# Attention of two batches in front of gate and val of batch 0, with gate and val weights fetched from memory for each batch

## The chip, the cores and the metric

The kernel runs on one core of one Trainium2 chip. The metric is device time in microseconds (us). PE is TensorE, DVE VectorE, ACT ScalarE, POOL GpSimd. A "record" is one entry of the trace; the 48 matmuls of gate and val of batch 0 stand there as 96 records. A line number such as L407 is a line of the kernel whose profile is shown; the same code has other numbers in other kernels: gate and val matmuls are L382 before and L407 after, the output projection of batch 0 is L468 and L493, the making of v L356 and L381, the first matmuls of batch 1 L420 and L445.

## The reference

Eight batches (8 heads, 512 positions, 64 wide) attend to 32 states each, and the states attend to the positions. The 544 rows of a batch go through RMS norm and a SwiGLU layer. The weights arrive in float64.

```
scores = scale * x @ state.T ; a = softmax(scores) ; xread = a @ state
a2 = softmax(scale * state @ x.T)                  ; sread = a2 @ x
x = concat(xread, sread)  -> rows of 512
xn = x / sqrt(mean(x*x) + 1e-6) * rms_g
out = (silu(xn @ w_gate) * (xn @ w_val)) @ w_out   # d_ff = 1536
```

## The kernel before

DVE and ACT turn the weights into float32, 18 pieces of 128x1024: twelve of gate and val (a gate and a val piece make a pair `mp`), six of w_out. For batch 0 the kernel multiplies the states into a pair of gate and val (`make_v`), then the attention weights into that (`hidden`, twelve tiles numbered from 0, also called hidden tiles, 3.5 us of PE each), then projects (`project_as_ready`, 42 us of PE). Batches 1 to 7 use seven products in place of eight. Attention is a generator; each `next` or `some(n)` emits its next steps, which end up between the other work.

```python
def to_float32(k):                      # 5 DVE and 3 ACT operations a piece (cut)
    ...
    VE.tensor_scalar(ex, hi, 20, 0x7ff, ...)              # L158
    VE.tensor_scalar(top, hi, 0xfffff, 0x100000, ...)     # L164
    VE.scalar_tensor_tensor(out=man, in0=top, ...)        # L165
    VE.scalar_tensor_tensor(out=ex, in0=hi, ...)          # L167
    VE.tensor_tensor(out=dst, in0=man, in1=ex, op=ALU.mult)   # L171

steps = attention(0)
while next(steps) != "tokens":
    pass
make_v(0, 0)
ready(4)                                # four pieces converted
for _ in steps:
    pass

for b in range(B):
    steps = attention(b + 1) if b + 1 < B else state_norm()
    if b == 0:
        for m in range(NM):
            if m % 2 == 0 and m + 2 < NM:
                make_v(b, m // 2 + 1)
            hidden(m, S, ...)
        def between(m):                 # called at even m of the projection
            some(5)
            if m == NM - 4:
                ready(len(pieces)); early.close(); open_late()
                some(20)
                prepare(b + 1)
        project_as_ready(store_tokens(b), between)
    else:
        ...                             # seven products (cut)
```

Of the kernel before, what the change touches and what calls it, by code (L numbers as in the profile page):

```python
# [8 lines left out]
F32 = mybir.dt.float32  # L9
# [7 lines left out]
P = 128  # L17
RAW_AHEAD = 4


@with_exitstack
def kernel(
# [35 lines left out]
    one = ctx.enter_context(tc.tile_pool(name="one", bufs=1))  # L58
    two = ctx.enter_context(tc.tile_pool(name="two", bufs=2))
    aps = ctx.enter_context(tc.tile_pool(name="aps", bufs=2, space=PSUM))  # L60
    vps = ctx.enter_context(tc.tile_pool(name="vps", bufs=2, space=PSUM))
# [19 lines left out]
    def load_x(b, queue):  # L81
        x_sb[b] = one.tile([P, NC, H * D], F32, name="x_b")
        for c in range(NC):
            queue.dma_start(
                out=x_sb[b][:, c].rearrange("p (h d) -> p h d", h=H),
                in_=x[b, :, P * c:P * c + P, :].rearrange("h p d -> p h d"))
# [4 lines left out]
    GE.memset(mhalf, -0.5)  # L91
    ones = consts.tile([P, P], F32, name="ones")
    GE.memset(ones, 1.0)
# [5 lines left out]

    w = consts.tile([P, NI, NM, 2, P], F32, name="w")  # L100
    wo = consts.tile([P, NM, DM], F32, name="wo")
# [4 lines left out]
    for mp in range(NM // 2):  # L106
        for k, dram in enumerate((moe_w_gate, moe_w_val)):
            pieces.append((w[:, :, 2 * mp:2 * mp + 2, k, :],
                           dram[:, 2 * P * mp:2 * P * mp + 2 * P].rearrange("(i p) f -> p i f", p=P)))
    for mp in range(NM // 2):  # L110
        pieces.append((wo[:, 2 * mp:2 * mp + 2].rearrange("p m (i f) -> p m i f", f=P),
                       moe_w_out[2 * P * mp:2 * P * mp + 2 * P].rearrange("(m p) f -> p m f", p=P)))
    raw = {}

    def load_piece(k):
        if k >= len(pieces):
            return
        dst, src = pieces[k]
        if src.dtype == F32:
            src = src.rearrange("p a (c f) -> p a c f", f=P)  # L120
            for a in range(src.shape[1]):
                nc.sync.dma_start(out=dst[:, a], in_=src[:, a])
            return
        raw[k] = raws.tile([P, 8 * P, 2], I32, name="raw")
        out_ = raw[k].rearrange("p (a f) two -> p a (f two)", a=src.shape[1])
        for a in parts(k):
            nc.sync.dma_start(out=out_[:, a], in_=src[:, a].bitcast(I32))

    def parts(k):

        n = pieces[k][1].shape[1]
        return (slice(0, n // 2), slice(n // 2, n)) if k == 0 else (slice(0, n),)
# [3 lines left out]
    def ready(n):  # L136

        nonlocal n_ready
        while n_ready < min(n, len(pieces)):
            to_float32(n_ready)  # L140
            n_ready += 1

    def to_float32(k):


        load_piece(k + RAW_AHEAD)
        if k not in raw:
            return
        whole = raw.pop(k)
        tops = conv.tile([P, 8 * P], I32, name="top")  # L150
        exs = conv.tile([P, 8 * P], I32, name="ex")
        n = pieces[k][1].shape[1]
        for a in parts(k):
            cols = slice(8 * P * a.start // n, 8 * P * a.stop // n)
            r, top, ex, dst = whole[:, cols, :], tops[:, cols], exs[:, cols], pieces[k][0][:, a]
            hi = r[:, :, 1]
            man = r.bitcast(F32)[:, :, 0]
            VE.tensor_scalar(ex, hi, 20, 0x7ff, op0=ALU.logical_shift_right, op1=ALU.bitwise_and)  # L158

            SE.activation(out=ex, in_=ex, func=ACTF.Relu, scale=-1.0, bias=bounds[:, 0:1])  # L160
            SE.activation(out=ex, in_=ex, func=ACTF.Relu, scale=-float(1 << 23),
                          bias=bounds[:, 1:2])
            SE.activation(out=man, in_=r.bitcast(U32)[:, :, 0], func=ACTF.Copy, scale=2.0 ** -52)
            VE.tensor_scalar(top, hi, 0xfffff, 0x100000, op0=ALU.bitwise_and, op1=ALU.bitwise_or)  # L164
            VE.scalar_tensor_tensor(out=man, in0=top, scalar=2.0 ** -20, in1=man,  # L165
                                    op0=ALU.mult, op1=ALU.add)
            VE.scalar_tensor_tensor(out=ex, in0=hi, scalar=-(1 << 31), in1=ex,  # L167
                                    op0=ALU.bitwise_and, op1=ALU.bitwise_or)
            man, ex = (t.rearrange("p (a c f) -> p a c f", f=P, c=dst.shape[2])
                       for t in (man, ex.bitcast(F32)))  # L170
            VE.tensor_tensor(out=dst, in0=man, in1=ex, op=ALU.mult)  # L171
# [15 lines left out]
    def attention(b):  # L187
        xb, packed = x_sb.pop(b), rows.pop(b)
        if b + 1 < B:
            load_state(b + 1)  # L190

        stT = two.tile([P, 4, Ns], F32, name="stT")
# [19 lines left out]
        for j in range(4):  # L212
            for e in range(2):
                TE.matmul(out=sp[e][Ns * j:Ns * j + Ns, :], lhsT=stT[D * e:D * e + D, j, :],  # L214
                          rhs=xT[j // 2][D * e:D * e + D, j % 2].rearrange("p c t -> p (c t)"),
                          start=True, stop=True)
        sS = one.tile([P, 2, NC, P], F32, name="sS", tag="sS")
        e2 = one.tile([P, 2, NC, P], F32, name="e2", tag="xT0")
        s2 = two.tile([P, 2], F32, name="s2")
# [9 lines left out]
        for cp in range(2):  # L229
# [11 lines left out]
            yield  # L241
        aT = one.tile([P, 2, NC, P], F32, name="aT")
        for cp in range(2):
# [32 lines left out]
        for c in range(NC):  # L276
            TE.matmul(out=sp[:, c:c + 1], lhsT=sq[0][:, 0, P * c:P * c + P], rhs=ones[:, 0:1],  # L277
                      start=True, stop=True)
# [3 lines left out]
        rp = inverse_rms(ss, NC)  # L282
        aT_s[b] = two.tile([P, 2, S], F32, name="aT_s")
        VE.tensor_tensor(out=aT_s[b], in0=aT.rearrange("p e c t -> p e (c t)"),
                         in1=rp.unsqueeze(1).to_broadcast([P, 2, S]), op=ALU.mult)
# [10 lines left out]
        yield  # L296
        e2T = one.tile([P, 2, NC, P], F32, name="e2T", tag="eS")
        for e in range(2):
# [17 lines left out]
        for e in range(2):  # L316
            VE.tensor_scalar(sr[:, D * e:D * e + D], rp[:, e, :], z2[:, e:e + 1], None,
                             op0=ALU.mult)
        if b + 1 < B:
            load_x(b + 1, nc.sync)  # L320
        tp = aps.tile([P, 4, Ns], F32, name="at")
# [4 lines left out]
    def state_norm():  # L326

        sq = one.tile([P, NI, NT], F32, name="sqT", tag="eS")
        SE.activation(out=sq, in_=xsT, func=ACTF.Square, scale=DM ** -0.5)
        sp = aps.tile([P, NT // P], F32, name="at")  # L330
        for r in range(NT // P):
            for i in range(NI):
                TE.matmul(out=sp[:, r:r + 1], lhsT=sq[:, i, P * r:P * r + P], rhs=ones[:, 0:1],
                          start=(i == 0), stop=(i == NI - 1))
        ss = two.tile([P, NT // P], F32, name="sst")
        VE.tensor_scalar(ss, sp, 1e-6, None, op0=ALU.add)
        rp = inverse_rms(ss, NT // P)
        for i in range(NI):
            VE.scalar_tensor_tensor(out=xsT[:, i, :], in0=xsT[:, i, :], scalar=rms_g[:, i:i + 1],
                                    in1=rp[:, 0:NT], op0=ALU.mult, op1=ALU.mult)  # L340
        yield
# [8 lines left out]
    def make_v(b, mp):  # L350

        ready(2 * mp + 2)
        pv = [vps.tile([P, 4 * P], F32, name="pv") for e in range(2)]
        for j in range(4):
            for e in range(2):
                TE.matmul(out=pv[e][Ns * j:Ns * j + Ns, :],  # L356
                          lhsT=stT_g[b][D * e:D * e + D, j, :],
                          rhs=w[D * e:D * e + D, j, 2 * mp:2 * mp + 2].rearrange(
                              "p m k f -> p (m k f)"),
                          start=True, stop=True)  # L360
        v = two.tile([P, 2, 2, 2, P], F32, name="v")
        for e in range(2):
# [229 lines left out]
    ready(4)  # L592
    for _ in steps:
        pass
# [4 lines left out]

    for b in range(B):  # L600
        steps = attention(b + 1) if b + 1 < B else state_norm()
        if b == 0:
            for m in range(NM):
                if m % 2 == 0 and m + 2 < NM:
                    make_v(b, m // 2 + 1)
                v, _ = v_sb[b, m // 2]
                hidden(m, S, lambda e, k: v[:, e, m % 2, k, :],
                       [aT_s[b][:, e, :] for e in range(2)])

            def between(m):  # L610
                some(5)
                if m == NM - 4:
                    ready(len(pieces))
                    early.close()
                    open_late()
                    some(20)
                    prepare(b + 1)

            project_as_ready(store_tokens(b), between)
            sums = weight_sums()  # L620
        else:
            pairs = [hidden_seven(b, mp) for mp in range(NM // 2)]
# [15 lines left out]
    for m in range(NM):  # L638
        hidden(m, NT, lambda i, k: w[:, i, m, k, :], [xsT[:, i, :] for i in range(NI)])
    project_seven(NT, store_states, lambda: None, lambda: None)  # L640
# [30 lines left out]
```

## Time and profile before

| | before |
|---|---|
| median time in the rounds with the changed kernel | 879.43 us (878.08 to 880.06, 4 runs) |
| PE busy | 827.5 of 877.2 us |
| PE idle before batch 1 (161.2 us) | 34.5 us |
| PE idle from batch 1 to the end (716.0 us) | 15.2 us |
| last piece of weights converted | 136.2 us |

"Busy" says that an engine had work, not that the work was fast: at a granted clock of 0.50 sixteen matmuls for v take 2.44 us, at 1.00 they take 1.09. The sum "idle plus extra busy" is therefore what a stage has lost, and it is used below. The main lines stand in the prediction. One view more is the list of PE's waits from 60 to 165 us (columns: total us, times, longest us). It names who ended each wait. Its first three lines are shown; the four left out are of 0.7 us and less:

```profile
PE f L382 <- ACT v L363: 5.5, 3, 2.4
PE at L277 <- DVE sq L274: 1.8, 1, 1.8
PE at L184 <- POOL ri L181: 0.8, 1, 0.8
```

The first line is the conversion arriving just in time: gate and val wait for v, which waits for weights. The other two are attention of batch 1, which runs between matmuls of the projection.

### The profile page before, as it was taken

How to read it: one execution, taken by the hardware profiler on the slowest of the kernel's cores; microseconds unless marked ns; L12 is line 12 of the kernel's file. 1: busy time of each engine (PE TensorE's matmuls, PEld its weight loads, DVE VectorE, ACT ScalarE, POOL GpSimd, SP SyncE). 2: the span in 40 equal slices, each digit the busy share in tenths (PEclk: the TensorE clock that was granted, in tenths of full speed). 3: DMA queues.
4: the chain of work that ended last, by engine and by line, in shares of the span. 5: the costliest groups of instructions: out<-in, count | busy, mean ns of one | idle time of the engine just before them, and what ended most of it. 6: DMA issues, size and time to landing. Idle time of an engine off the chain costs nothing.

```text
span 877.2 us, 11950 instructions
## 1 busy us (share of the span) xinstructions
PE 827.5 (94%) x4806; PEld 607.1 (69%) x4806; DVE 473.5 (54%) x749; ACT 341.2 (39%) x571; POOL 150.9 (17%) x215
## 2 busy tenths in 40 slices
PE   3598898999999999999999999999999999999998
PEld 2143343577877778777877787777877787788886
DVE  5889997269216941476226921694148623651231
ACT  5667771464125520562136412552056313520110
POOL 0000003131113211230123112221132022310000
PEclk9589999999999999999999999999999999999999
DMA  9455412100210002000200021001100000001000
GB/s 284 156 145 182 157 48 49 48 1 4 50 48 2 1 21 67 13 1 4 72 25 1 4 50 47 1 1 36 50 13 1 1 25 25 1 1 37 13 0 25
DMA packets 53815, 37.47 MB, mean 43 GB/s; under 512 B 37888, under 2 KB 45568, under 8 KB 53760
## 3 DMA queue, kind: packets, MB, share of 16 engines
q1 hardware_dynamic: 49600, 35.66, 13.9%
q10 hardware_dynamic: 4160, 1.05, 0.6%
q8 instruction: 38, 0.62, 0.3%
q14 instruction: 17, 0.14, 0.1%
HBM read 27.79 MB, written 8.91 MB: 42 GB/s over the span
## 4 chain that ended last, share of the span: by engine, by line
PE 72%; issue 11%; DVE 9%; ACT 5%; DMA 1%; POOL 0%; ACTq 0%; POOLq 0%
PE f L511 30%; PE f L420 24%; PE f L382 5%; PE pv L356 4%; PE f L468 2%; PE at L206 2%; ACT sq L270 1%; PE at L214 1%; ACT e L294 1%; PE at L277 1%; PE at L264 1%; DVE m L290 1%; DVE hb L450 1%; DVE hb L446 1%; DVE sq L273 1%
## 5 line engine op out<-in xcount | busy, mean ns | idle before, releaser
L420 PE MATMUL f<-aT_s,v 128*128 128x256 f32 x504 | 131.9, 393 | 2.8 <-ACT g L437 2.8
L511 PE MATMUL f<-wo,hb 128*128 128x256 f32 x540 | 128.5, 396 | 0.0
L420 PEld LDWEIGHTS f<-aT_s,v 128*128 128x128 f32 x504 | 89.4, 189 | 52.9 <-issue 29.8
L511 PEld LDWEIGHTS f<-wo,hb 128*128 128x128 f32 x540 | 107.0, 200 | 17.6 <-ACT ot L531 1.9
L531 ACT COPY ot<-f 128x256 f32<-128x256 f32 x60 | 19.6, 375 | 195.6 <-PE f L511 190.3
L363 ACT COPY v<-pv 128x512 f32<-128x512 f32 x96 | 51.7, 591 | 106.6 <-PE pv L356 106.6
L511 PE MATMUL f<-wt,hs 128*128 128x256 f32 x360 | 88.8, 392 | 0.0
L371 POOL TENSOR_TENSOR vs<-v 128x256 f32<-128x256 f32 x42 | 30.6, 730 | 330.5 <-ACT v L363 330.5
L420 PE MATMUL f<-aT_t,vs 128*128 128x256 f32 x336 | 86.3, 379 | 0.0
L435 DVE TENSOR_TENSOR g<-g,f 128x512 f32<-128x512 f32 x42 | 28.7, 683 | 90.2 <-PE f L420 72.1
L511 PEld LDWEIGHTS f<-wt,hs 128*128 128x128 f32 x360 | 65.2, 191 | 16.4 <-issue 4.9
L536 DVE TENSOR_TENSOR ot<-ot,f 128x256 f32<-128x256 f32 x45 | 17.0, 417 | 104.9 <-issue 53.5
L420 PEld LDWEIGHTS f<-aT_t,vs 128*128 128x128 f32 x336 | 63.8, 190 | 9.5 <-issue 0.8
L356 PE MATMUL pv<-w,stT_g 64*32 64x512 f32 x768 | 64.7, 619 | 4.0 <-ACT sq L270 2.7
L445 ACT ACTIVATE hb<-g 128x1024 f32<-128x1024 f32 x42 | 44.4, 1057 | 34.8 <-DVE g L439 34.8
L446 DVE SCALAR_TENSOR_TENSOR hb<-hb,g 128x1024 f32<-128x1024 f32 x42 | 51.5, 1225 | 7.6 <-ACT hb L445 7.6
L181 POOL TENSOR_TENSOR ri<-ss,mhalf 128x4 f32<-128x4 f32 x8 | 8.9, 1113 | 237.9 <-DVE ss L280 196.7
L382 PE MATMUL f<-aT_s,v 128*128 128x512 f32 x96 | 43.3, 604 | 5.5 <-ACT v L363 5.5
L468 PE MATMUL f<-wo,hb 128*128 128x512 f32 x96 | 43.5, 597 | 0.0
L420 PE MATMUL f<-aT_t,v 128*128 128x256 f32 x168 | 43.1, 379 | 0.0
L420 PE MATMUL f<-aT_s,vs 128*128 128x256 f32 x168 | 43.1, 379 | 0.0
L382 PE MATMUL f<-xsT,w 128*128 128x256 f32 x192 | 41.6, 379 | 0.0
(114 smaller groups left out, 1244.7 us busy)
## 6 DMA issues: line engine op xcount, KB each, us to landing
x_b<-in_x_dram SPq DMA_DIRECT2D x28, 256.0 KB, 4.4
out_dram<-ot SPq DMA_DIRECT2D x56, 128.0 KB, 1.8
raw<-in_moe_w_val_dram SPq DMA_DIRECT2D x6, 1024.0 KB, 5.3
raw<-in_moe_w_out_dram SPq DMA_DIRECT2D x6, 1024.0 KB, 4.7
raw<-in_moe_w_gate_dram SPq DMA_DIRECT2D x5, 1024.0 KB, 5.2
x_b<-in_x_dram ACTq DMA_DIRECT2D x4, 256.0 KB, 5.2
raw<-in_moe_w_gate_dram SPq DMA_DIRECT2D x2, 512.0 KB, 6.0
out_dram<-ot SPq DMA_DIRECT2D x4, 256.0 KB, 2.0
```

Source lines behind the costliest of these rows:

```text
L206: TE.transpose(out=tp[:, c, :], in_=xb[:, c, P * j:P * j + P], identity=ident)
L356: TE.matmul(out=pv[e][Ns * j:Ns * j + Ns, :], lhsT=stT_g[b][D * e:D * e + D, j, :], rhs=w[D * e:D * e + D, j, 2 * mp:2 * mp + 2].rearrange ...
L363: SE.copy(v[:, e].rearrange("p m k f -> p (m k f)"), pv[e])
L371: GE.tensor_tensor(out=vs[:, 0], in0=a21, in1=a22, op=ALU.add)
L382: TE.matmul(out=ps[:, 0:n], lhsT=lhs(i, k), rhs=r, start=(i == 0), stop=(i == len(rhs) - 1))
L420: TE.matmul(out=ps[:, i, :], lhsT=lhs[:, i, :], rhs=rhs, start=(start and i == 0), stop=True, skip_group_check=True)
L435: VE.tensor_tensor(out=g[:, :, 0, :], in0=g[:, :, 0, :], in1=ys, op=ALU.add)
L445: SE.activation(out=h, in_=gate, func=ACTF.Tanh, scale=0.5)
L446: VE.scalar_tensor_tensor(out=h, in0=h, scalar=1.0, in1=gate, op0=ALU.add, op1=ALU.mult)
L468: TE.matmul(out=op, lhsT=hb[:, m, P * r:P * r + P], rhs=wo[:, m, :], start=(m == 0), stop=(m == NM - 1))
L511: TE.matmul(out=ps[:, r, :], lhsT=lhs(k)[:, P * r:P * r + P], rhs=rhs(k), start=(start and r == 0 and k == 0), stop=(k == HM - 1), skip_gr ...
L531: SE.copy(kept[r], ps[:, r, :])
```

## The change

The intent: PE idles in the first 100 us while DVE converts, so the attention of batch 1 goes there, where it would take nothing from the projection. To make room on the chip's memory, gate and val no longer stay resident: each converted pair is stored once to device memory, and each later use fetches it again into one of three buffers. The core of the diff:

```diff
+W_BUFS = 3
-    w = consts.tile([P, NI, NM, 2, P], F32, name="w")
+    w_d = [scratch.tile([P, NI, 2, 2, P], F32, name="w_d%d" % mp) for mp in range(NM // 2)]
+    def fetch(n):
+        if NM // 2 <= n < (B + 1) * (NM // 2):
+            nc.sync.dma_start(out=new_w(n), in_=w_d[n % (NM // 2)])
     ...                                  # in ready(), after a val piece:
+            if k < NM and k % 2:
+                nc.sync.dma_start(out=w_d[k // 2], in_=w_sb[k // 2])
     ...                                  # in make_v(), after its matmuls:
+        fetch(b * (NM // 2) + mp + W_BUFS)
     ...                                  # attention: x and scores double, own tiles for exp
     ready(4)
-    for _ in steps:
-        pass
+    states_read = steps
+    steps = attention(1)
+    for _ in states_read:
+        pass
+    while next(steps) != "tokens":
+        pass
     ...
                 hidden(m, S, ...)
+                next(steps, done)
     ...
             def between(m):
-                some(5)
                 if m == NM - 4:
                     ready(len(pieces)); early.close(); open_late()
-                    some(20)
                     prepare(b + 1)
```

The pair's use in the last stage (`hidden` for the state rows) fetches in the same way.

More of the change, by code (lines that the diff above doesn't have):

```diff
@@ L59 @@
     two = ctx.enter_context(tc.tile_pool(name="two", bufs=2))
+    ws = ctx.enter_context(tc.tile_pool(name="ws", bufs=W_BUFS))
+    scratch = ctx.enter_context(tc.tile_pool(name="scratch", bufs=1,
+                                             space=bass.MemoryType.DRAM))
     aps = ctx.enter_context(tc.tile_pool(name="aps", bufs=2, space=PSUM))
@@ L81, in load_x @@
     def load_x(b, queue):
-        x_sb[b] = one.tile([P, NC, H * D], F32, name="x_b")
+        x_sb[b] = two.tile([P, NC, H * D], F32, name="x_b")
         for c in range(NC):
@@ L91 @@
     GE.memset(mhalf, -0.5)
-    ones = consts.tile([P, P], F32, name="ones")
+    ones = consts.tile([P, 1], F32, name="ones")
     GE.memset(ones, 1.0)
@@ L97 @@
     rms_g = consts.tile([P, NI], F32, name="rms_g")
-    w = consts.tile([P, NI, NM, 2, P], F32, name="w")
+    w_d = [scratch.tile([P, NI, 2, 2, P], F32, name="w_d%d" % mp) for mp in range(NM // 2)]
+    w_sb = {}
     wo = consts.tile([P, NM, DM], F32, name="wo")
@@ L106, with new_w, home @@
     for mp in range(NM // 2):
-        for k, dram in enumerate((moe_w_gate, moe_w_val)):
-            pieces.append((w[:, :, 2 * mp:2 * mp + 2, k, :],
-                           dram[:, 2 * P * mp:2 * P * mp + 2 * P].rearrange("(i p) f -> p i f", p=P)))
+        for dram in (moe_w_gate, moe_w_val):
+            pieces.append(dram[:, 2 * P * mp:2 * P * mp + 2 * P].rearrange("(i p) f -> p i f", p=P))
     for mp in range(NM // 2):
-        pieces.append((wo[:, 2 * mp:2 * mp + 2].rearrange("p m (i f) -> p m i f", f=P),
-                       moe_w_out[2 * P * mp:2 * P * mp + 2 * P].rearrange("(m p) f -> p m f", p=P)))
+        pieces.append(
+            moe_w_out[2 * P * mp:2 * P * mp + 2 * P].rearrange("(m p) f -> p m f", p=P))
     raw = {}
+    def new_w(n):
+        w_sb[n] = ws.tile([P, NI, 2, 2, P], F32, name="w_m")
+        return w_sb[n]
+    def fetch(n):
+        if NM // 2 <= n < (B + 1) * (NM // 2):
+            nc.sync.dma_start(out=new_w(n), in_=w_d[n % (NM // 2)])
+    def home(k):
+        if k >= NM:
+            m = 2 * (k - NM)
+            return wo[:, m:m + 2].rearrange("p m (i f) -> p m i f", f=P)
+        mp = k // 2
+        return (w_sb[mp] if k % 2 else new_w(mp))[:, :, :, k % 2, :]
     def load_piece(k):
@@ L117, in load_piece @@
             return
-        dst, src = pieces[k]
+        src = pieces[k]
         if src.dtype == F32:
-            src = src.rearrange("p a (c f) -> p a c f", f=P)
-            for a in range(src.shape[1]):
-                nc.sync.dma_start(out=dst[:, a], in_=src[:, a])
             return
@@ L129, in parts @@
     def parts(k):
-        n = pieces[k][1].shape[1]
+        n = pieces[k].shape[1]
         return (slice(0, n // 2), slice(n // 2, n)) if k == 0 else (slice(0, n),)
@@ L139, in ready @@
         while n_ready < min(n, len(pieces)):
-            to_float32(n_ready)
+            k = n_ready
+            to_float32(k)
+            if k < NM and k % 2:
+                nc.sync.dma_start(out=w_d[k // 2], in_=w_sb[k // 2])
             n_ready += 1
@@ L146, in to_float32 @@
         load_piece(k + RAW_AHEAD)
+        to = home(k)
         if k not in raw:
+            src = pieces[k].rearrange("p a (c f) -> p a c f", f=P)
+            for a in range(src.shape[1]):
+                nc.sync.dma_start(out=to[:, a], in_=src[:, a])
             return
@@ L151, in to_float32 @@
         exs = conv.tile([P, 8 * P], I32, name="ex")
-        n = pieces[k][1].shape[1]
+        n = pieces[k].shape[1]
         for a in parts(k):
             cols = slice(8 * P * a.start // n, 8 * P * a.stop // n)
-            r, top, ex, dst = whole[:, cols, :], tops[:, cols], exs[:, cols], pieces[k][0][:, a]
+            r, top, ex, dst = whole[:, cols, :], tops[:, cols], exs[:, cols], to[:, a]
             hi = r[:, :, 1]
@@ L190, in attention @@
             load_state(b + 1)
+            load_x(b + 1, nc.sync)
         stT = two.tile([P, 4, Ns], F32, name="stT")
@@ L216, in attention @@
                           start=True, stop=True)
-        sS = one.tile([P, 2, NC, P], F32, name="sS", tag="sS")
-        e2 = one.tile([P, 2, NC, P], F32, name="e2", tag="xT0")
+        sS = two.tile([P, 2, NC, P], F32, name="sS")
+        e2 = one.tile([P, 2, NC, P], F32, name="e2")
         s2 = two.tile([P, 2], F32, name="s2")
@@ L241, in attention @@
             yield
-        aT = one.tile([P, 2, NC, P], F32, name="aT")
+        aT_s[b] = two.tile([P, 2, S], F32, name="aT_s")
+        aT = aT_s[b].rearrange("p e (c t) -> p e c t", c=NC)
         for cp in range(2):
@@ L276, in attention @@
         for c in range(NC):
-            TE.matmul(out=sp[:, c:c + 1], lhsT=sq[0][:, 0, P * c:P * c + P], rhs=ones[:, 0:1],
+            TE.matmul(out=sp[:, c:c + 1], lhsT=sq[0][:, 0, P * c:P * c + P], rhs=ones,
                       start=True, stop=True)
@@ L282, in attention @@
         rp = inverse_rms(ss, NC)
-        aT_s[b] = two.tile([P, 2, S], F32, name="aT_s")
-        VE.tensor_tensor(out=aT_s[b], in0=aT.rearrange("p e c t -> p e (c t)"),
+        VE.tensor_tensor(out=aT_s[b], in0=aT_s[b],
                          in1=rp.unsqueeze(1).to_broadcast([P, 2, S]), op=ALU.mult)
@@ L296, in attention @@
         yield
-        e2T = one.tile([P, 2, NC, P], F32, name="e2T", tag="eS")
+        e2T = one.tile([P, 2, NC, P], F32, name="e2T")
         for e in range(2):
@@ L318, in attention @@
                              op0=ALU.mult)
-        if b + 1 < B:
-            load_x(b + 1, nc.sync)
         tp = aps.tile([P, 4, Ns], F32, name="at")
@@ L332, in state_norm @@
             for i in range(NI):
-                TE.matmul(out=sp[:, r:r + 1], lhsT=sq[:, i, P * r:P * r + P], rhs=ones[:, 0:1],
+                TE.matmul(out=sp[:, r:r + 1], lhsT=sq[:, i, P * r:P * r + P], rhs=ones,
                           start=(i == 0), stop=(i == NI - 1))
@@ L350, in make_v @@
     def make_v(b, mp):
-        ready(2 * mp + 2)
+        ready(2 * mp + 2 if b == 0 else 0)
+        w = w_sb.pop(b * (NM // 2) + mp)
         pv = [vps.tile([P, 4 * P], F32, name="pv") for e in range(2)]
@@ L357, in make_v @@
                           lhsT=stT_g[b][D * e:D * e + D, j, :],
-                          rhs=w[D * e:D * e + D, j, 2 * mp:2 * mp + 2].rearrange(
-                              "p m k f -> p (m k f)"),
+                          rhs=w[D * e:D * e + D, j].rearrange("p m k f -> p (m k f)"),
                           start=True, stop=True)
+        fetch(b * (NM // 2) + mp + W_BUFS)
         v = two.tile([P, 2, 2, 2, P], F32, name="v")
@@ L600 @@
     for b in range(B):
-        steps = attention(b + 1) if b + 1 < B else state_norm()
-        if b == 0:
+        if b > 0:
+            steps = attention(b + 1) if b + 1 < B else state_norm()
+        else:
             for m in range(NM):
@@ L620 @@
             sums = weight_sums()
-        else:
+        if b > 0:
             pairs = [hidden_seven(b, mp) for mp in range(NM // 2)]
@@ L638 @@
     for m in range(NM):
-        hidden(m, NT, lambda i, k: w[:, i, m, k, :], [xsT[:, i, :] for i in range(NI)])
+        n = B * (NM // 2) + m // 2
+        hidden(m, NT, lambda i, k: w_sb[n][:, i, m % 2, k, :], [xsT[:, i, :] for i in range(NI)])
+        if m % 2:
+            fetch(n + W_BUFS)
     project_seven(NT, store_states, lambda: None, lambda: None)
```

## The prediction

> **What bounds the kernel now.** I read the page first: TensorE (PE) is busy 827.5 of 877.2 us, so a change of order can win back at most the other 50 us and what a low clock costs. The row of slices says where these lie: in the first seven of 40 slices (22 us each), before batch 1 starts.
>
> ```profile
> PE   3598898999999999999999999999999999999998
> DVE  5889997269216941476226921694148623651231
> PEclk9589999999999999999999999999999999999999
> ```
>
> From slice 8 on PE is full, and the waits of PE from 165 us to the end sum to only 10.5 us (7.7 for the sum of squares, six times, and 2.8 for a copy of ScalarE). There the kernel is bound by PE work, and the change leaves that work as it is. So only the start can change, and I cut it in stretches of 10 us (columns: window, PE, PE weight loads, DVE, ACT, POOL, granted clock, DMA share, GB/s):
>
> ```profile
> 20.00:30.00 10.00, 2.06 (x8) 1.43 (x8) 10.00 (x17) 7.29 (x9) 0.00 (x0) 0.63 0.48 168
> 30.00:40.00 10.00, 5.95 (x35) 0.92 (x34) 8.86 (x11) 7.83 (x11) 0.00 (x0) 0.50 0.50 153
> ...
> 60.00:70.00 10.00, 10.00 (x38) 3.96 (x37) 10.00 (x14) 8.37 (x11) 0.00 (x0) 1.00 0.43 127
> 70.00:80.00 10.00, 8.44 (x38) 3.50 (x37) 10.00 (x14) 7.53 (x10) 0.00 (x0) 1.00 0.55 193
> 80.00:90.00 10.00, 7.78 (x38) 3.38 (x37) 10.00 (x14) 6.72 (x10) 0.00 (x0) 1.00 0.59 210
> ```
>
> The reader is to see DVE at 10.00 of 10 while PE is not: from about 20 us to 136 us VectorE is the limit, because it turns the 64-bit weights into float32. PE is idle 24 us before 50 us and 10.5 us between 50 and 160 us (10 minus PE, summed over the windows). The order of time on PE and DVE shows how the two are coupled:
>
> ```profile
> 75.95 7.13 PE L382 MATMUL f<-aT_s,v 128*128 128x512 f32 x16 [1.56 <-ACT v L363]
> ...
> 99.18 7.13 PE L382 MATMUL f<-aT_s,v 128*128 128x512 f32 x16 [2.36 <-ACT v L363]
> ...
> 147.36 14.00 PE L468 MATMUL f<-wo,hb 128*128 128x512 f32 x32
> 161.20 1.03 PE L420 MATMUL f<-aT_s,v 128*128 128x256 f32 x4
> ```
>
> ```profile
> 134.97 1.22 DVE L171 TENSOR_TENSOR wo<-raw,ex 128x1024 f32<-128x1024 f32 x1
> ```
>
> The gate and val matmuls (L382) wait for v, which is made just in time from weights just converted. The last piece is converted at 136.2 us; PE, which has fallen behind, ends batch 0 at 161.2 us. That last time is what I predict; everything after it takes 877.2 - 161.2 = 716 us in both.
>
> **What the Trainium skill says.** (1) "TensorE: Matmul & The Clock Gate", Part 1: the clock halves after about one idle window of 3.4 us and returns after about as long of busy time. The trace agrees: PE is idle from 19.5 to 27.2 us, the clock is 0.79 at 22 to 23 us, then 0.50 until 49 to 50 us (0.56), when PE has been busy without a break since 40 us: a return later than the page says. (2) "VectorE: DVE Perf Modes", Mode 2x_2P: a tensor-scalar on float32 can pass two elements a cycle, an operation on two tensors one. The trace agrees: 128x1024 takes 683 ns in L158 and 1213 ns in L165. So the two-tensor operations of the conversion don't get cheaper by a new output layout. (3) "DMA: Bandwidth & Descriptors", the SWDGE table: 1 MB takes 6.15 us. Here a 1 MB load of raw weights takes 4.7 to 5.3 us (median, issue to landing, another queue); I use that.
>
> **The change part by part.**
>
> Traffic: six 1 MB stores of converted gate and val, and 48 fetches of 1 MB (six for each of batches 1 to 7 and the state rows), 56.6 MB on top of 37.5 MB. In batches 1 to 7 the making of v comes every 8 to 10 us (162.2, 172.1, 180.3, 189.4, 198.3 us), and a fetch is issued three ahead: about 25 us for 5. In the last stage a pair of hidden tiles is 32 records of 128x256, spaced 216 ns, 6.9 us; a fetch has two pairs, 13.8 us. All hidden: 0 us. DMA is at 0 to 2 tenths there.
>
> Conversion and attention, VectorE: no operation is added. Spacing of starts is 0.60 us (L158, L164, and 512-wide operations) and 1.135 us (1024-wide on two tensors), so a piece costs 2 x 0.60 + 3 x 1.135 = 4.6 us, 18 pieces 83 us; 12 pairs on hidden tiles 14.4 us; an attention 10.7 us. Measured to 136.2 us: 118.6 us of work and 17.6 us of gaps (10 of them for the first loads).
>
> What moves: attention of batch 1 runs in before at 74 to 146 us between other work, mostly in the shadow of the output projection (L468), which is why it costs PE only 3.4 us of gaps there (10 minus 7.46 and 9.16). In the changed build the order of instructions puts it behind the first eight gate and val matmuls; the other 40 come after its reads. All of its VectorE work is then in front of the conversion of the last gate and val pieces. The two softmax chains cannot overlap work of PE: only hidden tiles 0 and 1 (7 us), two makings of v (2 us) and about 11 us of attention work are there between 53 us and its end.
>
> How long is that chain? Attention of batch 0 takes 35 us from stT (11.4) to the scaled aT_s (46.4). In the changed order 30 us of VectorE work stands between the same two points of batch 1. Waits are added where little stands between a send and a return: for exp (0.6 us of work in between), for the squares (6.9 us against a chain of 7.0 to 8), for the row sum and the reciprocal (2.3 us against 4 to 5; batch 0 waits 2.88 and 1.49 us there). I estimate 5 to 8 us of new gaps, 7 taken. So from about 54 us the chain ends near 88 to 91 us.
>
> Then I count back. VectorE's end of conversion: 118.6 + 2.3 (the tail of attention 1 that before has behind it) + 17.6 + 7 = 145.5 us. After the last gate and val piece the new order leaves six pieces of w_out and six hidden pairs, less one early operation: 27.6 + 7.2 - 0.6 = 34.2 us. That piece is ready at 111.3 us (95.7 in before). Just before it VectorE does hidden tiles 4 and 5, so PE is done with tile 5 at 104 to 107 us. From there PE is the limit with no gap: hidden tiles 6 to 11, 48 records at 0.4375 us = 21.0; three makings of v, 3.1; the projection, 96 records = 42.0; in all 66.1 us. End of batch 0: 170 to 173 us against 161.2, that is 9 to 12 us later. PE idle in all: more in 60 to 100 us (some 17 us), less afterwards (the 3.4 us in the projection and the waits for v at 99 us are gone).
>
> Sum: +10 us, 878.96 to 889 us.
>
> **The rivals.** (a) *The early attention fills PE's hole and shortens the start.* For it: PE is idle 34.5 us before batch 1. Against it: the hole is caused by VectorE, whose work only gets a chain in front of it; the same attention stood under 42 us of projection before, where it was nearly free. If the new gaps are only 2 us and PE packs well, the end of batch 0 is at 164 to 165, 882 us; a gain would need PE to have less idle than 34.5 us, for which I see little: at most 870 us. (b) *The clock.* If PE waits more than some 3 us at a time between 60 and 90 us, it falls to 0.50 and 10 to 15 us of its work doubles; the chain is lengthened by some 3 to 8 us. That would give 892 to 897 us. For it: it happened in attention of batch 0. Against it: PE also has hidden tiles to do. (c) *A new wait for the buffers.* Three buffers for six pairs in batch 0: the fourth to sixth conversion wait for a making of v and a store, and the prefetch for batch 1 takes two of the three early. The sixth pair reuses the fifth's place (or one freed as late), but stands 10 us behind it on VectorE against a store of some 5 us. If it waits anyway, some 2 to 6 us more. (d) *Fetches late in every batch.* One us at each of 48 would make 48 us; the slack of 20 us speaks against it.
>
> **Range and chances.** Middle 889. Low end: rival (a)'s mild form and less, 880. High end: the clock and some buffer wait together, 900. Faster by 2% (under 861) would need 17 us less idle in a start that got one more chain: 0.02. Slower by 2% (over 896.5) needs +17.6 us, which (b) and (c) together could make: 0.16. Within 2%: 0.82.
>
> **What would show it.** Batch 1's first matmul pair of the seven-product form (L420 before, 161.2 us) starts at 170 to 173 us, and from there to the end 716 us as before. PE is idle some 15 us and more in 55 to 100 us, at or near full after about 105 us. VectorE ends its last conversion at 143 to 148 us. No wait of PE for a fetch above 1 us. DMA moves 94 MB. Wrong would make it: fetch waits in later batches; a start of batch 1 before 161 us; gaps of VectorE after 55 us summing to under 2 or over 15 us.

## More of the kernel before

The order on each engine is fixed when the kernel is built.

## The result, and the profile after

The changed kernel takes 889.85 us (median of 4 runs, 888.57 to 892.82) against 879.43 us. The ratio is 1.0125, 95% interval 1.0096 to 1.0155.

The page's slices of the changed kernel, 22 us each (rows of PE, DVE and clock):

```profile
PE   3477999999999999999999999999999999999997
DVE  4897999068514762369216931685147623661131
PEclk9585999999999999999999999999999999999999
```

PE's row is full from the fifth slice on, before only from the eighth, and yet the time is longer. Only the third and fourth slice and the clock (5 in the fourth) hint at it; the windows of 10 us show what happened (columns: window, PE, PE weight loads, DVE, ACT, POOL, granted clock, DMA share, GB/s):

```profile
60.00:70.00 10.00, 2.70 (x15) 1.72 (x14) 10.00 (x22) 8.01 (x13) 0.00 (x0) 0.72 0.67 213
70.00:80.00 10.00, 5.95 (x38) 1.51 (x39) 9.09 (x11) 7.95 (x12) 0.00 (x0) 0.50 0.40 118
80.00:90.00 10.00, 10.00 (x37) 4.84 (x36) 4.62 (x7) 4.16 (x6) 1.92 (x1) 0.58 0.86 308
```

PE has 2.70 and 5.95 us of work in two windows in which the kernel before had 10.00 and 8.44, and the clock is down to half until 88 us, where it was full before. In the third window DVE, the converter, is busy only 4.62 of 10 us: it now waits for PE. The order of time on PE (columns: start, duration, what, and in brackets the idle time just before and what ended it):

```profile
60.27 1.31 PE L259 MATMUL at<-ident,sS 128*128 128x128 f32 x8
68.00 1.09 PE L281 MATMUL at<-ident,eS 128*128 128x128 f32 x4 [6.41 <-DVE eS L276]
...
76.35 2.44 PE L381 MATMUL pv<-w_m,stT_g 64*32 64x512 f32 x16 [2.66 <-ACT sq L297]
...
98.75 7.13 PE L407 MATMUL f<-aT_s,v 128*128 128x512 f32 x16
...
114.92 14.00 PE L407 MATMUL f<-aT_s,v 128*128 128x512 f32 x32
...
158.53 14.00 PE L493 MATMUL f<-wo,hb 128*128 128x512 f32 x32
172.36 1.03 PE L445 MATMUL f<-aT_s,v 128*128 128x256 f32 x4
```

and on DVE:

```profile
83.74 0.16 DVE L307 TENSOR_SCALAR ss<-at 128x4 f32<-128x4 f32 x1 [2.55 <-PE at L304]
...
88.47 1.22 DVE L310 TENSOR_TENSOR aT_s<-aT_s,at 128x1024 f32<-128x1024 f32 x1 [2.83 <-PE at L209]
...
107.63 2.35 DVE L196 TENSOR_TENSOR w_m<-raw,ex 128x1024 f32<-128x1024 f32 x2
...
143.86 1.22 DVE L196 TENSOR_TENSOR wo<-raw,ex 128x1024 f32<-128x1024 f32 x1
```

Batch 1 starts at 172.4 us against 161.2, and from there to the end it takes 716.4 us against 716.0. The whole loss is in the start: 11.2 us. PE idle before batch 1 went from 34.5 to 39.6 us (5.1 more), and PE's busy time went from 827.5 to 833.6 us (6.1 more, for the same 4806 matmuls: the half clock). Together that is 11.2.

The memory traffic rose to 94.11 MB from 37.47 MB; the 48 fetches land in 4.8 us (median), and PE never waits for one. PE's waits from batch 1 to the end are the same two kinds as before, 7.7 and 2.8 us:

```profile
PE at L304 <- DVE sq L301: 7.7, 6, 1.3
PE f L445 <- ACT g L462: 2.8, 12, 0.2
```

### The profile page after: what moved, and what is told of

Its sections match the earlier page's. It is cut to its first block, busy times and chain, and to the rows that moved or that the text cites. A ratio compares the mean times of both kernels' runs of the same rounds, so it can differ in the third digit from the quotient of the medians. Undisturbed runs are those within 1.5% of the kernel's fastest.

```text
span 888.8 us, 12039 instructions
## 1 busy us (share of the span) xinstructions
PE 833.6 (94%) x4806; PEld 610.8 (69%) x4806; DVE 474.7 (53%) x749; ACT 342.1 (38%) x571; POOL 151.3 (17%) x215
## 2 busy tenths in 40 slices
DMA packets 61592, 94.11 MB, mean 106 GB/s; under 512 B 38752, under 2 KB 46432, under 8 KB 54624
## 4 chain that ended last, share of the span: by engine, by line
PE 78%; DVE 12%; ACT 6%; DMA 2%; issue 1%; SPq 0%; POOL 0%; ACTq 0%; DVEq 0%
PE f L536 29%; PE f L445 24%; PE f L407 7%; PE pv L381 5%; PE f L493 4%; PE at L232 2%; ACT sq L297 2%; PE at L240 1%; PE at L291 1%; PE at L304 1%; ACT e L320 1%; DVE m L316 1%; DVE sq L300 1%; PE at L327 1%; DVE hb L475 1%
## 5 line engine op out<-in xcount | busy, mean ns | idle before, releaser
L445 PE MATMUL f<-aT_t,vs 128*128 128x256 f32 x336 | 86.3, 379 | 0.0
L460 DVE TENSOR_TENSOR g<-g,f 128x512 f32<-128x512 f32 x42 | 28.7, 683 | 95.6 <-PE f L445 72.7
L381 PE MATMUL pv<-w_m,stT_g 64*32 64x512 f32 x768 | 65.7, 628 | 6.0 <-ACT sq L297 5.3
L470 ACT ACTIVATE hb<-g 128x1024 f32<-128x1024 f32 x42 | 44.4, 1057 | 34.5 <-DVE g L464 34.5
L407 PE MATMUL f<-aT_s,v 128*128 128x512 f32 x96 | 45.8, 620 | 0.0
L407 PE MATMUL f<-xsT,w_m 128*128 128x256 f32 x192 | 41.6, 379 | 0.0
L464 DVE TENSOR_TENSOR g<-g,f 128x512 f32<-128x512 f32 x42 | 28.4, 676 | 23.9 <-PE f L445 23.9
```

Source lines behind the costliest of these rows:

```text
L381: TE.matmul(out=pv[e][Ns * j:Ns * j + Ns, :], lhsT=stT_g[b][D * e:D * e + D, j, :], rhs=w[D * e:D * e + D, j].rearrange("p m k f -> p (m k ...
L407: TE.matmul(out=ps[:, 0:n], lhsT=lhs(i, k), rhs=r, start=(i == 0), stop=(i == len(rhs) - 1))
L445: TE.matmul(out=ps[:, i, :], lhsT=lhs[:, i, :], rhs=rhs, start=(start and i == 0), stop=True, skip_group_check=True)
L460: VE.tensor_tensor(out=g[:, :, 0, :], in0=g[:, :, 0, :], in1=ys, op=ALU.add)
L464: VE.tensor_tensor(out=g[:, :, 1, :], in0=g[:, :, 1, :], in1=zs, op=ALU.add)
L470: SE.activation(out=h, in_=gate, func=ACTF.Tanh, scale=0.5)
```

## The experiments

Three theories were to be told apart. A: the place of the attention costs, because its chain stands bare: PE, DVE and ACT hand it to each other and PE has little else to do meanwhile. B: the trip through memory and the three buffers cost. C: the place costs, but not because the chain is bare: any attention work on DVE in front of the last weights delays them. Beside these stood the clock, as a cause of its own. Eleven kernels ran, each correct.

**e1_memory_only: the memory trip alone.** The changed kernel with attention of batch 1 put back into the projection.

```diff
-    states_read = steps
-    steps = attention(1)
-    for _ in states_read: ...
-    while next(steps) != "tokens": ...
+    for _ in steps: pass
     ...
+                some(5)                    # and some(20), as before
```

> Gate and val through memory with three buffers as in the change, but attention of batch 1 back in the projection of batch 0 as before. Theory A (the loss is the place of the attention alone): 878 to 881 us, batch 1's first product of seven starts at 161 to 162 us, no wait of TensorE for a fetch. Rival B (fetches, stores and the three buffers cost): 884 to 890 us. If the two halves share, 882 to 885.

Measured: 881.37 us, before 879.60 us, ratio 1.0026 (1.0004 to 1.0048). No wait for a fetch. The profiled run was the slowest of its six (885.06 us); in it batch 1 starts at 168.2 us and the rest takes 715.0 us. So the trip costs some 2 us, by this profile in front of batch 1, and the larger part of the loss must come from elsewhere. The expected start of 161 to 162 us was missed.

**e2_front_only: the early attention alone.** Weights resident. To find the room, the attention's tiles share memory, the exp for the states' reads is written over the scores, and x, which has two buffers, is loaded earlier.

```diff
-        e2 = one.tile([P, 2, NC, P], F32, name="e2", tag="xT0")
-        eS = one.tile([P, NC, 2, 4, Ns], F32, name="eS", tag="eS")
+        e2 = sS
+        eS = one.tile([P, NC, 2, 4, Ns], F32, name="eS", tag="xT0")
     ...                                    # likewise sq, e2T; aT becomes aT_s; two x buffers
+    states_read = steps                    # attention(1) in front, as in the change
```

> Weights resident as before, no memory trip, but attention of batch 1 in front as in the change (tags of the attention's tiles shared to find the room, order on TensorE as in the change). Theory A: 887 to 892 us, batch 1 starts at 171 to 174 us, clock 0.50 somewhere between 60 and 90 us. Rival B: 878 to 882 us.

Measured: 886.72 us, ratio 1.0084 (1.0069 to 1.0099). Batch 1 starts at 173.9 us, as late as in the changed kernel, though no weight leaves the chip. The same hole is there, with the same length:

```profile
68.75 1.09 PE L256 MATMUL at<-ident,eS 128*128 128x128 f32 x4 [6.43 <-DVE eS L251]
...
107.94 7.13 PE L381 MATMUL f<-aT_s,v 128*128 128x512 f32 x16
115.00 1.09 PE L355 MATMUL pv<-w,stT_g 64*32 64x512 f32 x16
116.02 14.00 PE L381 MATMUL f<-aT_s,v 128*128 128x512 f32 x32
```

(f at L381 are gate and val tiles.) The start alone would have made it 12.7 us slower. It is only 7.4, because the stretch from batch 1 to the end took 710.8 us, not 716: a gain that I had not expected, and that needed a control.

**e8_tags_only: the control.** The tile changes of e2_front_only, with attention of batch 1 in the projection as before.

> The control for e2_front_only and the two spread runs: their tile changes alone (exp of the state's reads written over the scores, shared tags, two x buffers), weights resident, attention of batch 1 in the projection as in the kernel before. In those three runs the stretch from batch 1 to the end took 709 to 711 us against 716 of the kernel before. If the tile changes did that: 872 to 875 us, batch 1 starts at 160 to 163 us, and the front place alone then costs e2_front_only 12 us. If the early attention did it: 878 to 881 us.

Measured: 875.38 us, ratio 0.9951 (0.9936 to 0.9966). Batch 1 starts at 163.3 us and the rest takes 710.8 us. So the tile changes alone gain 0.5%, and against this control the early place costs 1.0084 / 0.9951 = 1.0134, which is 11.7 us. This is theory A or C, not B.

**e7_spread0 and e7_spread4: attention early, but not bare.** As e2_front_only, with two steps of attention of batch 1 after every gate and val tile of batch 0, from the first tile or from the fifth. In e7_spread4 all steps that are left run after the last tile.

```diff
+    steps = attention(1)                   # not run through at once
     ...
                 hidden(m, S, ...)
-                next(steps, done)
+                some(2)                    # e7_spread4: from m = 4 on
```

> As e2_front_only, but attention of batch 1 is spread over the gate and val tiles of batch 0, two steps after each of the twelve, so that TensorE has hidden tiles to do in each of its waits. Theory A in the form 'the chain stands bare, and TensorE waits and loses its clock': 875 to 881 us, batch 1 starts at 157 to 163 us, clock at 1.00 from 50 us on. Rival C ('any attention work of VectorE in front of the conversion of the last weights delays the start, bare or not'): 885 to 890 us.

> The same spread, begun only after the fifth gate and val tile. Theory A: 876 to 882 us, near the kernel before and near e7_spread0. Rival C: between, 882 to 886 us.

Measured: 876.47 us (0.9963, interval 0.9947 to 0.9979) and 878.23 us (0.9985, 0.9971 to 0.9998). Against the control that is 1.1 us (not clear of noise, the intervals overlap) and 3.0 us, where the front place costs 11.7. The start of batch 1, at 165.1 and 167.1 us, came later than I had expected of e7_spread0 (157 to 163); the control's own start is 163.3. Nor did the clock stay at 1.00: in e7_spread0 it was 0.50 from 95 to 100 us and 0.64 and 0.67 in the two windows from 110 to 120 us.

This pair with e2_front_only shows the cause. In both the last gate and val piece is ready at almost the same time, first e2_front_only and then e7_spread0:

```profile
110.99 1.23 DVE L171 TENSOR_TENSOR w<-raw,ex 128x1024 f32<-128x1024 f32 x1
```

```profile
108.47 2.35 DVE L171 TENSOR_TENSOR w<-raw,ex 128x1024 f32<-128x1024 f32 x2
```

112.2 us and 110.8 us. But PE's order of time in e7_spread0 after that is short:

```profile
110.89 1.50 PE L355 MATMUL pv<-w,stT_g 64*32 64x512 f32 x16 [2.19 <-DVE w L171]
...
115.14 7.73 PE L381 MATMUL f<-aT_s,v 128*128 128x512 f32 x14
122.71 27.63 PE L467 MATMUL f<-wo,hb 128*128 128x512 f32 x64
...
165.13 1.03 PE L419 MATMUL f<-aT_s,v 128*128 128x256 f32 x4
```

Only 16 gate and val records (two tiles) are left, while e2_front_only still has part of tiles 6 and 7 and then 32 records, 14 us, before its projection starts at 129.9 us against 122.7. Conversion ends at almost the same time too (146.9 and 145.7 us), and in the control at 136.9 us; so the delay of the conversion does not cost what theory C says. The control shows it for gate and val too: there the last piece is ready at 95.3 us, 15.5 us before that of e7_spread0, and batch 1 starts only 1.8 us earlier.

```profile
94.05 1.21 DVE L171 TENSOR_TENSOR w<-raw,ex 128x1024 f32<-128x1024 f32 x1
```

What costs is that PE stood idle while tiles whose weights were ready waited behind the attention in its order. In e2_front_only the second pair of weights (tiles 2 and 3) is converted at 39.1 us and the third (tiles 4 and 5) at 59.9 us, by DVE's order of time, and PE begins tile 2 at 86.3 us:

```profile
37.85 1.22 DVE L171 TENSOR_TENSOR w<-raw,ex 128x1024 f32<-128x1024 f32 x1
...
58.65 1.22 DVE L171 TENSOR_TENSOR w<-raw,ex 128x1024 f32<-128x1024 f32 x1
```

```profile
86.25 2.07 PE L381 MATMUL f<-aT_s,v 128*128 128x512 f32 x2
```

PE's time before batch 1 says the same, and it sets the clock aside for this pair:

| | start of batch 1 | PE idle before it | PE busy before it |
|---|---|---|---|
| e8_tags_only (control) | 163.3 us | 33.8 us | 129.6 us |
| e7_spread0 | 165.1 us | 30.9 us | 134.3 us |
| e2_front_only | 173.9 us | 39.8 us | 134.1 us |

Both early versions are busy equally long, 4.6 to 4.7 us longer than the control, so both lost clock; the 8.8 us between them are idle time alone. Against the control the front place costs 6.0 us of idle time and 4.6 us of slower matmuls. C keeps 1 to 3 us at most.

**e13_late: the other direction.** The control with no step of attention of batch 1 before the fifth tile of the projection.

```diff
-                some(5)
+                some(5 if m >= 4 else 0)
```

> e8_tags_only with attention of batch 1 begun later: no step before the fifth tile of the output projection. If the front place costs because its work on VectorE stands before weights that TensorE waits for, later is no worse: 872 to 876 us, conversions end earlier by 2 to 6 us. If the end of the projection then waits for the chain: 877 to 882 us, with TensorE idle before batch 1.

Measured: 874.65 us, ratio 0.9944 (0.9928 to 0.9959). Conversion ends at 129.4 us, 7.5 us before that of the control, and batch 1 starts at 162.0 us. So 7.5 us of earlier conversion bring about 1 us. Only w_out came earlier, though: the last gate and val piece is ready at 96.1 us, in the control at 95.3. What this run shows is that the end of the conversion, which is that of w_out, is not the bound. PE is the bound, by the work it has left; that agrees with the pair above.

**e4_warm1 and e11_warm_more: the clock.** The changed kernel with matmuls that nobody reads put into PE's waits in attention of batch 1, to keep the clock up: six after the scores, and in e11_warm_more one after the exp and four after the reads as well.

```diff
+            if b in WARM and cp == 1:
+                warm = vps.tile([P, S], F32, name="pv")
+                for k in range(WARM[b]):
+                    TE.matmul(out=warm, lhsT=ident, rhs=sS[:, k % 2]..., start=True, stop=True)
```

> The changed kernel with six matmuls that nobody reads in TensorE's wait of 6.4 us in attention of batch 1, so that its clock does not halve there. If half the loss is the clock (as TensorE's busy time, 6 us up, suggests): 885 to 888 us, no long run of 0.50 between 65 and 90 us, batch 1 starts at 168 to 170 us. If the chain's waits for VectorE and ScalarE alone set it: 889 to 892 us.

> The changed kernel with unread matmuls in three of TensorE's waits in attention of batch 1 (six after the scores, one after the exp, four after the reads), since in e4_warm1 the clock still fell at 74 us. If the clock lies on the path: no half-speed matmul between 62 and 90 us (16 of the v matmuls in 1.1 us, not 2.4), batch 1 starts at 167 to 170 us, 884 to 887 us. If the waits of the chain and VectorE's queue set the end: 888 to 892 us and batch 1 at 171 to 174 us though the clock is full.

Measured: e4_warm1 890.97 us (1.0132, 1.0111 to 1.0153), e11_warm_more 887.22 us (1.0089, 1.0076 to 1.0102). In e4_warm1 the clock still fell at about 74 us, so it settles little. In e11_warm_more PE's lines show the v matmuls at 1.51 us in place of 2.44, so the half clock is mostly gone, and the next line is the new hole:

```profile
76.61 1.51 PE L401 MATMUL pv<-w_m,stT_g 64*32 64x512 f32 x16
80.45 1.28 PE L324 MATMUL at<-ones,sq 128*128 128x1 f32 x8 [2.34 <-DVE sq L321]
```

The scaled attention weights begin at 84.6 us, 3.9 us earlier than in the changed kernel, and still batch 1 starts at 172.5 us. The added matmuls took 11.1 us of PE, the builder had moved gate and val tiles behind them, and so PE had as much left as before. The total is some 3 us lower by the ratios (their intervals overlap), but the profile puts this behind batch 1, where nothing was edited: 713.3 us against 716.4. There the mean clock is below 1.00 (0.98) in three of six stretches (one of 80 us, five of 96), in the changed kernel's profile in five; each such stretch is worth, by estimate, some 2 us (2% of 96). So the added matmuls did not move the start; how much the half clock costs by itself stays open, since every way I had to keep it up also changed the order and gave PE more to do.

**e5_before_warm0: the same in batch 0 of the kernel before.** Seven such matmuls in the wait of 7.7 us.

> The kernel before with seven matmuls that nobody reads in the wait of 7.7 us in attention of batch 0. If the half clock from 23 to 50 us lies on the path: 875 to 878 us, batch 1 starts at 157 to 160 us. If VectorE's conversion sets the start whatever the clock: 878 to 880 us.

Measured: 880.77 us, ratio 1.0016 (0.9996 to 1.0036): no gain. The clock fell a little later and was at 0.50 from 30 to 50 us. The wait was not filled to its end (2.58 us were left), so this too only says that a few unread matmuls are no remedy.

**e12_exp_in_place: what the control gained from.** The changed kernel with `e2 = sS` as its only edit, so that the exp must come after the other reads of the scores.

> The changed kernel with one edit of e8_tags_only: the exp for the state's reads is written over the scores, so it has to come after the other reads of them. If that order on ScalarE is what shortened the stretch from batch 1 to the end in e8_tags_only: that stretch takes 711 us (716 in the changed kernel), TensorE's 2.8 us of waits for a copy of g are gone, batch 1 starts at 171 to 174 us, 884 to 886 us in all. If another of the tile changes did it: 888 to 892 us.

Measured: 885.47 us, ratio 1.0072 (1.0059 to 1.0085). Batch 1 starts at 174.8 us, the rest takes 709.6 us, and PE's waits there are one kind less:

```profile
PE at L304 <- DVE sq L301: 8.5, 6, 1.4
```

The 2.8 us behind ACT's copy of g are gone: ACT no longer does the long exp just in front of that copy. That edit gives the gain of the tile changes. PE's idle time in the stretch fell by only 2.0 us (15.7 to 13.7), and the rest of the 6.8 us is shorter busy time, which goes with fewer stretches at a lowered clock (two of six, not five); whether those are an effect of the order or chance was not tested.

**e10_memory_four: why the memory trip costs 2 us.** e1_memory_only with `W_BUFS = 4`.

> As e1_memory_only (memory trip, attention in the projection), with four buffers for gate and val in place of three. If its 2 us came from conversions that wait for a buffer: 878 to 880 us, no wait of VectorE for TensorE at the sixth pair. If they came from the extra traffic or the order: 880 to 883 us.

Measured: 881.95 us, ratio 1.0032 (1.0016 to 1.0049). A fourth buffer takes nothing away. In both profiles PE waits 1.6 us for DVE's copy of the next batch's states, because the built order has the scores of batch 1 before the last gate and val tiles; and loads of raw val weights land in 8.2 and 8.0 us, where they took 5.3 in the kernel before. Which of these makes the 2 us is open. With the attention in front the trip costs nothing that can be seen: e12_exp_in_place (with it) is at 1.0072, e2_front_only (without it) at 1.0084; but these two differ in some tile changes as well.

**A version that beats both.** e13_late (ratio 0.9944) and e8_tags_only (0.9951) are faster than both kernels, by 0.5% against the kernel before; their intervals overlap.

## Why the prediction was right

- *Where it is decided.* Right: the time from batch 1 to the end was called the same, 716 us, and was 716.4. The start of batch 1 was called 170 to 173 us, and was 172.4; the total 889, and was 889.85.
- *The chain of VectorE.* Right: 7 us of new gaps were called; the gaps after 54 us sum to 7.1 us (0.91 + 2.55 + 2.83 + 0.27 + 0.19 + 0.35). The two large ones stand at the row sum and the reciprocal, as forecast; none stands at the exp or the squares. The chain was to end near 88 to 91 us; aT_s begins at 88.5. The last gate and val piece was called at 111.3 us and ready at 110.0, the end of conversion 145.5 and was 145.1.
- *The count back.* It reached the right time: PE was done with tile 5 at 105.9 us (called 104 to 107), and from there to batch 1 it took 66.5 us (called 66.1). But VectorE was not the limit up to there, as the count has it: PE is busy from 79.5 us on with gaps of 0.8 us in all, not only from about 105 us. And it reads the loss as a matter of conversion ("the hole is caused by VectorE, whose work only gets a chain in front of it"), and that is not the lever. With conversion ending as late as in e2_front_only, e7_spread0 starts batch 1 8.8 us earlier; with the conversion of w_out 7.5 us earlier than in the control, e13_late starts it 1.3 us earlier. The lever is a term that I used and did not question: six hidden tiles still to do when the last weights come. It is large because PE's order held tiles back, not because their weights were missing.
- *"The two softmax chains cannot overlap work of PE."* True of this order, wrong as a reason: e7_spread0 overlaps them with the tiles and costs 1.1 us more than the control, not 11.7.
- *The size of PE's idle time.* Too large: "some 17 us" in 60 to 100 us, measured 11.5; the sign "15 us and more in 55 to 100 us" failed. In its place came 6.1 us of busy time at half clock, which I had set apart as rival (b) with 3 to 8 us on top. The two errors cancelled in the sum, and that is luck. One reason can be read off: the 7 us of gaps leaned on the waits of batch 0 (2.88 and 1.49 us), and these stood at a clock of 0.50 to 0.51 themselves, so that part of (b) was already counted. That the clock itself delays the start was not shown: e11_warm_more took the half clock mostly away and the start stayed.
- *Rivals (c) and (d).* No late fetch, right. No visible buffer wait in the changed kernel, right, though a store took 9.1 us and not some 5. In e1_memory_only the trip costs 2 us, which the prediction had at 0.

## What to carry to other kernels

To fill an engine's idle time it is not enough to put work there: ask whether the new work is itself a chain that makes the engine wait, and what ready work its fixed order then holds back. Spread such a chain in small steps between independent work, and judge a stage by what the bound engine still has to do when the last input arrives, not by when that input arrives. And run the control for everything that an experiment had to change on the side; here it was worth more than the change.

## What the Trainium skill lacked or had wrong

- "TensorE: Matmul & The Clock Gate", Part 1, says that about 3.4 us of busy time bring the clock back. In the kernel before PE was busy from 38.6 us on and the clock returned at 49 to 50 us, after some 11 us; in the changed kernel busy from 79.5 us, and back near 88 us. In e11_warm_more it did come back after about 3.4 us (half clock from about 67.5 to 70.9 us and from 81.1 to 84.5 us, estimates from the mean clock of windows of 1 us). Much of the work in the slow cases is transposes and small matmuls; the same page says of transposes that they do not count as busy in the same way, and no run here separates the two. The page names an idle window of about 3.4 us for the fall as well. Here shorter waits were enough: 2.18 and 2.34 us at those two places. In e5_before_warm0, where seven unread matmuls in the wait of 7.7 us put the fall off from about 23 to about 30 us, the longest wait before the fall was 2.58 us.
- The same page warns that clock events in a trace are not to be trusted fully. In e7_spread0 the record shows 1.00 from 20 to 50 us, while 16 matmuls for v took 2.44 us there, as in the runs with 0.50 on record, and 1.09 us later. The durations are the better witness.
- "DMA: Bandwidth & Descriptors", Bandwidth, the measured table, has 6.15 us for a 1 MB load on another kind of queue. Here a 1 MB fetch takes 4.8 us from issue to landing (median of 48). The page's table has no store: 1 MB to memory took 9.1 us (median of 6, beside other loads).
